# Attention and a gated feed-forward layer in two passes: two ff tiles moved to the second pass, with one pair of weights fetched again

## The chip, the cores and the metric

The kernel runs on one core of a Trainium2 chip. The metric is the device time of one launch in microseconds; three runs of the kernel before took 961.78, 963.28 and 963.41 us, with a median of 963.28 us.

## The reference

Causal attention with a window of 128 and a slope per head on q, k and v of shape (8, 8, 576, 64), whose output becomes 4608 rows of 512; then two matrix products with a gate between them. The weights come as float64.

```python
B, H, S, D = q.shape                              # 8, 8, 576, 64
scores = np.matmul(q, k.transpose(0, 1, 3, 2)) / np.sqrt(D)
bias = slopes[:, None, None] * (-np.abs(rel))[None]
scores = np.where((rel >= 0) & (rel < 128), scores + bias[None], -1e9)
attn = np.exp(scores - scores.max(-1, keepdims=True))
attn = attn / (attn.sum(-1, keepdims=True) + 1e-09)
x = np.matmul(attn, v).transpose(0, 2, 1, 3).reshape(B * S, H * D)
h = x @ w_in                                      # 512 by 2048
sp = np.maximum(h, 0.0) + np.log1p(np.exp(-np.abs(h)))
out = (h * erf(sp)) @ w_out                       # 2048 by 512
```

## The kernel before

The 4608 rows are cut into 12 chunks of 384 (`CH`), the 2048 columns of the ff dimension into 16 tiles of 128 (an ff tile, `f`). Matrix products of the second part are made of three products of rounded halves (high by high, high by low, low by high), so that each logical 128x128 product is three matmuls.

**Attention.** A unit is one chunk and two heads, 48 in all (`Attention.unit`). Its steps, each on the engine named: the scores on PE (L478, 24 matmuls on quarters of the array, 64 by 64); the bias, with a running minimum, on DVE (L505); the exponentials and their sums on ACT (L515); the inverse of the sums on DVE (L528, L529); the scaling on POOL (L538); the transposes on PE (L554); the copies of these to `pT` on DVE or ACT (L417, L415). For two units together the products with v are made on PE (L595, on quarters of the array too); they are rounded to the high half of `x` on DVE or ACT, and the rest is the low half, on DVE (L605). `save_x` writes `x` to DRAM (L776). In every third chunk (two remainders of 192 rows) the scores are four groups of heads and blocks of rows; there they go to three banks, with a drain of PE before the last group (L474, L475).

**First pass.** It makes ff tiles 0 to 5 (`NF1 = 6`) for each chunk as soon as its x is there, between the steps of the attention. One first-pass unit is one chunk and one ff tile, 72 in all: 12 matmuls to the bank `h` (L801), the copy to `hs` (L784, L786), and 9 matmuls to the banks `o` (L864). Two units (`UPR = 2`) make a round (`flush`): ACT loads the softplus table, then the erf table, then the table of the exponentials (L832, L834, L835); DVE multiplies, rounds and takes the rest (L843, L848). After a chunk's last tile its three sums are copied (L786) and parked in DRAM (L878).

**Second pass.** The ten ff tiles left are five pairs. Two chunks are taken together, so that there are six double chunks. A pair of tiles and a double chunk is a 2 by 2 product of blocks, made with seven block products instead of eight (`pair`, L1003, 42 matmuls, from sums and differences of x and of the weights) and 36 matmuls to six banks (L1074). `operands` loads x again and makes the sums (L918 to L936); `store` adds the sum of the first pass and writes the output (L886, L891).

**Weights.** `plain` turns float64 to float32 with integer operations on ACT and DVE (L636 to L649). The first pass's tiles are prepared into SBUF (`prepare`); those of the second pass are prepared during the attention as well, eleven tiles of 256 KB for a pair, and parked in DRAM (`spare_pair`, `spare_out`, buffers `wd`). When the attention's buffers are closed (`close`, L1136), they are fetched (`fetch`, L724) into the room that these leave, and into that of the first pass's weights (`take`).

**What sets the order.** Every step is an `op` with a due time `at`, a cost and the engines that can do it. `Plan.run` plays the program through with these costs and writes the instructions out in the order that comes of it: on each engine, the ready step with the earliest due time goes next (L292). `unit_time` gives the due time of an attention unit, `t0 + U * TM` that of a first-pass unit, `t1 + p * TP` that of a pair. The tables `UNITS`, `FIRST`, `TILES` and `KEPT` shift single steps. The order of each queue, SP's with the DMAs too, is therefore fixed before the run.

**PSUM.** Before there are four kinds of banks: three (`a`) for scores, transposes and products with v, two (`h`), and three (`o0` to `o2`), one for each 128 rows of a chunk. In the second pass `a` and `o` together hold the six sums.

```python
                for o in ready[e]:
                    if o.ready > t + self.WAIT[e] + 1e-9 or (best and (best.at, best.seq) < (o.at, o.seq)):
                        continue
                    if fits(o) and all(t + o.costs[e] <= max(free[x], t) + c for x, c in o.costs.items()):
                        best = o
```

Of the kernel before, what the change touches and what calls it, by code (L numbers as in the profile page):

```python
# [8 lines left out]
F32 = mybir.dt.float32  # L9
# [10 lines left out]
P = 128  # L20
# [22 lines left out]
TE, NE = 4, 6  # L43
TA = 6.5
LL, LN, LT, PXL = 26, 0, 0, 0.1
SQ = 0.36
LEAD = 45

TM = 4.8
TP = 13.0  # L50
XL = 60
MC, MP, MH = 4, 16, -16
W1A, W1B, W1C = 24, 6, 0.3
W2A, W2B, W2C = 40, 2.0, 0.5
WS, WSD, NWH = 140, 34, 2
HM, LM, PM = 0.2, 1.5, 0.4
W1R, NSV, GSV = 40, 5, 3
XP2, XD2 = 24, 4
TS, VL, NQF, SLP = 9, 8, 4, True
WB, PIE = "o1", 2  # L60
VE = -17
TURN = (0, 1, 2, 1, 2, 1, 2, 1)

UNITS = {16: 8, 17: 8, 18: 4, 19: 4, 20: 4, 21: 4, 22: 4, 23: 4, 24: 4, 25: 4, 26: 4, 27: 4, 28: 4, 29: 4, 31: 4, 10: -4, 11: -4, 12: -2, 13: -4, 14: -4, 15: 4, 7: -8, 8: -8, 9: -8, 37: 1, 38: 1, 39: 1, 40: 1, 41: 1, 42: 1, 43: 1, 44: 1}
FIRST = {41: -8, 67: 1, 68: 1, 69: 1, 70: 1, 71: 1, 52: -8, 2: 4, 3: 4, 4: 4, 5: 4, 6: 4, 7: 4, 8: 4, 9: 4, 10: 4, 11: 4, 12: 4, 13: 4, 14: 4, 15: 4, 16: 4, 17: 4}
TILES = {(0, 4): -2, (0, 5): -2, (1, 0): -2, (1, 1): -2, (1, 3): -2, (1, 4): -2, (1, 5): -2}
KEPT = {(1, 11): 12, (1, 12): 12, (1, 13): 12, (1, 14): 12, (1, 15): 12, (1, 8): -3}
# [47 lines left out]
class Plan:  # L115
# [15 lines left out]
    def __init__(self):  # L131
        self.ops = []
        self.slots = {}

    def op(self, costs, emit, r=(), w=(), at=0.0, moved=0, packet=0.0, after=0.0, rows=1.0, count=0, tail=0.0, port=False):
        o = Op()
        o.count, o.tail, o.packet, o.after, o.port, o.landed = count, tail, packet, after, port, False
        o.rows = rows
        o.costs, o.emit, o.at, o.seq, o.moved, o.lag = costs, emit, at, len(self.ops), moved, 0.0
# [30 lines left out]
    def run(self):  # L170
# [12 lines left out]
        placed = set()  # L183

# [17 lines left out]
        def on_pe(o, t):  # L202

            left = o.costs["PE"]
# [57 lines left out]
        while events:  # L262
# [92 lines left out]
def unit_time(u):  # L355
    return TE * min(u, NE) + TA * max(0, u - NE) + UNITS.get(u, 0)

# [859 lines left out]
```

## Time and profile before

| | |
|---|---|
| median of three runs | 963.28 us |
| the profiled execution, its own time | 963.49 us |
| its span | 961.6 us (1.9 us less than its time) |
| PE busy | 942.8 us, 98% of the span |
| DVE busy | 685.5 us, 71% |
| ACT busy | 662.2 us, 69% |
| POOL busy | 160.0 us, 17% |
| attention, from its first scores to its last product with v | 5.8 to 414.3 us |
| rest of the first pass alone | 414.3 to 476.0 us |
| second pass | 476.0 to 956.4 us |

The span runs from the first to the last instruction that the profile shows; the time of an execution holds 1.9 us more. A share of busy time is an average over stages: DVE's 71% is over 90% in the attention and near 56% in the second pass. The start of an instruction is measured, while the end of a matmul is modelled and runs into the next one; so what a group of matmuls costs is read from its start to the start of the next.

### The profile page before, as it was taken

How to read it: one execution, taken by the hardware profiler on the slowest of the kernel's cores; microseconds unless marked ns; L12 is line 12 of the kernel's file. 1: busy time of each engine (PE TensorE's matmuls, PEld its weight loads, DVE VectorE, ACT ScalarE, POOL GpSimd, SP SyncE). 2: the span in 40 equal slices, each digit the busy share in tenths (PEclk: the TensorE clock that was granted, in tenths of full speed). 3: DMA queues.
4: the chain of work that ended last, by engine and by line, in shares of the span. 5: the costliest groups of instructions: out<-in, count | busy, mean ns of one | idle time of the engine just before them, and what ended most of it. 6: DMA issues, size and time to landing. Idle time of an engine off the chain costs nothing.

```text
span 961.6 us, 18491 instructions
## 1 busy us (share of the span) xinstructions
PE 942.8 (98%) x6872; PEld 820.6 (85%) x6872; DVE 685.5 (71%) x1641; ACT 662.2 (69%) x1247; POOL 160.0 (17%) x300
## 2 busy tenths in 40 slices
PE   8799999999999999999999999999999999999997
PEld 7677887888888888799999899998989898989996
DVE  6999999989999897966474475556458267544533
ACT  6899889878988897977764644645463545465551
POOL 4623442433432343400000000000000000000000
PEclk9999999999999999999999999999999999999999
DMA  9743366678775575469554414225134052220302
GB/s 354 265 147 137 119 240 210 224 249 283 237 275 207 189 255 209 145 241 391 201 206 142 165 45 154 98 99 165 56 142 153 12 197 79 86 99 22 110 1 77
DMA packets 63082, 160.73 MB, mean 167 GB/s; under 512 B 7056, under 2 KB 11280, under 8 KB 62992
## 3 DMA queue, kind: packets, MB, share of 16 engines
q1 hardware_dynamic: 62848, 159.41, 47.2%
q8 instruction: 55, 0.90, 0.4%
q14 instruction: 35, 0.29, 0.1%
q10 hardware_dynamic: 144, 0.13, 0.1%
HBM read 107.35 MB, written 52.17 MB: 166 GB/s over the span
## 4 chain that ended last, share of the span: by engine, by line
PE 86%; DVE 9%; DMA 2%; ACT 2%; issue 1%; POOL 0%; DVEq 0%; ACTq 0%; POOLq 0%
PE o L864 13%; PE pa L1003 13%; PE h L801 13%; PE po L1074 13%; PE pa L1074 12%; PE pc L1003 7%; PE s L478 4%; PE px L595 4%; PE t L554 4%; PE pb L1003 3%; DVE p L505 2%; ACT p L515 1%; DVE pT L417 1%; DVE gl L848 1%; PE warm_ps L410 1%
## 5 line engine op out<-in xcount | busy, mean ns | idle before, releaser
L538 POOL TENSOR_SCALAR p<-p,st 128x192 f32<-128x192 f32 (+1 forms) x288 | 157.0, 564 | 243.3 <-DVE st L529 171.9
L801 PE MATMUL h<-x,wi 128*128 128x384 f32 x864 | 174.9, 346 | 0.8 <-ACT hs L784 0.8
L784 ACT COPY hs<-pa 128x384 f32<-128x384 f32 x92 | 44.1, 480 | 180.2 <-PE pa L1003 179.6
L801 PEld LDWEIGHTS h<-x,wi 128*128 128x128 f32 x864 | 151.6, 190 | 9.3 <-issue 3.1
L864 PE MATMUL o<-wo,gh 128*128 128x512 f32 x432 | 141.6, 409 | 0.0
L515 ACT ACTIVATE p<-p,st 128x192 f32<-128x192 f32 (+1 forms) x288 | 123.9, 432 | 16.9 <-DVE st L505 16.7
L1003 PE MATMUL pa<-t,p 128*128 128x384 f32 x540 | 108.9, 336 | 0.0
L1003 PEld LDWEIGHTS pa<-t,p 128*128 128x128 f32 x540 | 96.4, 188 | 5.9
L786 DVE COPY hs<-pa 128x384 f32<-128x384 f32 x28 | 15.6, 557 | 108.8 <-PE pa L1003 108.8
L1074 PE MATMUL po<-ho,gh 128*128 128x512 f32 x270 | 91.0, 391 | 0.0
L1074 PE MATMUL pa<-ho,gh 128*128 128x512 f32 x270 | 90.5, 389 | 0.0
L864 PEld LDWEIGHTS o<-wo,gh 128*128 128x128 f32 x432 | 74.9, 188 | 15.4 <-issue 6.1
L864 PE MATMUL o<-wo,gl 128*128 128x512 f32 x216 | 85.3, 395 | 0.0
L554 PE MATMUL t<-ident,p 128*128 128x128 f32 x400 | 64.5, 280 | 7.8 <-POOL p L538 5.0
L1014 DVE TENSOR_TENSOR hs<-pc,hs 128x384 f32<-128x384 f32 x60 | 33.3, 555 | 53.7 <-PE pc L1003 39.4
L1074 PE MATMUL po<-ho,gl 128*128 128x512 f32 x180 | 71.3, 396 | 0.0
L1054 DVE TENSOR_TENSOR hs<-s,hs 128x768 f32<-128x768 f32 x60 | 56.2, 950 | 20.9 <-ACT s L1046 20.9
L1074 PE MATMUL pa<-ho,gl 128*128 128x512 f32 x180 | 70.1, 389 | 0.0
L505 DVE CUSTOM_DVE_ANT_0 p<-s,bias 128x192 f32<-128x192 f32 x224 | 65.8, 349 | 1.4 <-PE s L478 1.0
L554 PEld LDWEIGHTS t<-ident,p 128*128 128x128 f32 x400 | 47.3, 142 | 22.2 <-POOL p L538 11.0
L478 PE MATMUL s<-qk 64*64 64x192 f32 (+1 forms) x1152 | 58.9, 323 | 4.2 <-issue 1.7
L1074 PEld LDWEIGHTS pa<-ho,gh 128*128 128x128 f32 x270 | 50.7, 188 | 10.9
(258 smaller groups left out, 1836.4 us busy)
## 6 DMA issues: line engine op xcount, KB each, us to landing
xd<-x SPq DMA_DIRECT2D x24, 768.0 KB, 4.8
qk<-qk_a SPq DMA_DIRECT2D x32, 416.0 KB, 4.6
pd<-ot SPq DMA_DIRECT2D x36, 256.0 KB, 3.5
out<-pd SPq DMA_DIRECT2D x36, 256.0 KB, 3.6
p<-wd SPq DMA_DIRECT2D x35, 256.0 KB, 5.2
wri<-w_in SPq DMA_DIRECT2D x16, 512.0 KB, 6.6
wro<-w_out SPq DMA_DIRECT2D x16, 512.0 KB, 4.4
qk<-qk_c SPq DMA_DIRECT2D x16, 512.0 KB, 4.4
```

The costliest lines, as they stand in the source:

```text
L478: nc.tensor.matmul(bank[h * D : (h + 1) * D, x : x + n], lhsT=q(t, j, h), rhs=k(j, off[h], n), start=True, stop=True)
L505: nc.vector.tensor_tensor_reduce(out=pt[:, c0:, j, :], in0=ps[j][0][:, ps[j][1] : ps[j][1] + n].rearrange("p (c d) -> p c d", d=D), in1=se ...
L515: nc.scalar.activation(dst, dst, AF.Exp, bias=low[t][:, j : j + 1], scale=-1.0, accum_out=sums[t][:, j : j + 1])
L538: nc.gpsimd.tensor_scalar(dst, dst, sums[t][:, j : j + 1], 1.0, op0=ALU.mult, op1=ALU.mult)
L554: nc.tensor.matmul(two[:, :, (2 - cb) * D : (3 - cb) * D], lhsT=p[t][:, cb].rearrange("p j d -> p (j d)"), rhs=self.ident[:, :], is_transp ...
L595: nc.tensor.matmul(px[j][cols, to : to + m * D], lhsT=v[rows, blk, :], rhs=pT[rows, src : src + 4 * m - 3 : 4, :], start=x == 0, stop=x + ...
L784: self.nc.scalar.copy(out, src)
L801: nc.tensor.matmul(ps[:, :CH], lhsT=ww[:, cs], rhs=xx[:, k], start=(k2 + k + n == 0), stop=(k2 + k + n == 4),)
L864: nc.tensor.matmul(po.all, lhsT=g[:, j, cs], rhs=w.all, start=(u["start"] and n == 0), stop=(u["end"] and n == 2),)
L1003: nc.tensor.matmul(dst[:, :CH], lhsT=wv[i](k), rhs=xb[l][:, k], start=start and k + n == 0, stop=k + n == 3, skip_group_check=not start)
L1054: op({"DVE": dve(2 * CH)}, lambda e, s=s, hs=hs: V.tensor_tensor(hs.all, s.all, hs.all, ALU.mult), r=[s, *parts], w=parts, at=at, port=True)
L1074: nc.tensor.matmul(po.all, lhsT=g[:, k, cs], rhs=w.all, start=start and n == 0, stop=end and n == 2)
```

## The change

- Four ff tiles stay in the first pass (48 units) and twelve go to the second (six pairs). A round is a chunk's four units (`UPR = 4`), and the products to `o` go by 128 rows: for each `t` both pairs of tiles, six matmuls in one step.
- There is room in SBUF for five pairs' weights. Pair 5 shares that of pair 2 (`TURNS`): in each double chunk pair 5's eleven tiles are fetched after pair 2 is done, and from the second on pair 2's again (`again`), `WF` ahead of their due time.
- Scores, transposes, products with v and `o` share one pool of six banks. The scores of the last chunk of three have a fourth bank, and the drain is gone.
- The planner takes scores and products with v that follow such a step up to `QB` earlier, and counts the change of the array's mode (`SQ`) only where it happens. The due times are new; the four tables are replaced by `SHIFT`.

```diff
-NF1 = 6
-FITP, FITO = 3, 5
-UPR = 2
+NF1 = 4
+FITP, FITO = 3, 9
+TURNS = {5: 2}
+UPR = 4
+NA, KO = 6, 2
...
-LEAD = 45
+QB = 20
+LEAD = 54
-TM = 4.8
-TP = 13.0
+TM = 7.45
+TP = 14.65
...
-            left = o.costs["PE"]
+            left = o.costs["PE"] + (SQ if o.quad and not inside else 0)
...
+                due = lambda o: (o.at - (QB if o.quad and inside else 0), o.seq)
                 for o in ready[e]:
-                    if o.ready > t + self.WAIT[e] + 1e-9 or (best and (best.at, best.seq) < (o.at, o.seq)):
+                    if o.ready > t + self.WAIT[e] + 1e-9 or (best and due(best) < due(o)):
...
-        ps = [bank(j) for j in range(2 + (last and len(ts) == 3))]
+        ps = [Buf(self.ps, [P, 512], F32, "a", NA, f"s{u}_{j}", keep=0) for j in range(4 if last else 2)]
...
-            for step, row in enumerate(zip(*todo)):
-                if len(ps) == 3 and step == 2:
-                    nc.tensor.drain()
+            for t, put, off, n in todo:
                 for h in range(2):
...
-            po = [Buf(self.ps_o, [P, DM], F32, f"o{t}", 1, f"o{t}_{self.U}") for t in range(NTT)]
+            po = [Buf(self.ps_a, [P, DM], F32, "a", NA, f"o{t}_{self.U}", keep=KO) for t in range(NTT)]
...
-            for j, u in enumerate(us):
-                self.products(u, j, gh, gl)
+            done.append((us, gh, gl))
         for t in range(NTT):
+            for us, gh, gl in done:
+                self.products(us, t, gh, gl)
...
+                if j in TURNS or (c and j in TURNS.values()):
+                    weights.again(j, time(c * npair + j) - WF)
                 self.pair(c, j, weights, x, new, at)
...
-    for j in range(npair):
+    own = [j for j in range(npair) if j not in TURNS]
+    for j in own:
         homes[2, j] = [take(j < FITP, f"p{j}_{i}") for i in range(7)]
...
+    def again(j, at):
+        i = TURNS.get(j, j)
+        homes[2, j] = [Buf(pool2, [P, DM], F32R, f"p{i}_{n}", 1, f"p{j}_{n}") for n in range(7)]
+        for k in range(2):
+            homes[1, NF1 + 2 * j + k] = [Buf(pool2, [P, DM], F32R, f"{x}o{NF1 + 2 * i + k}", 1, f"{x}o{NF1 + 2 * j + k}") for x in "hl"]
+        fetch(j, at, [gone])
```

How the change moves instructions, at three places, as the two programs hold them (names are tiles, with their buffer numbers; `x2` is two instructions alike).

ACT, one round of the first pass in the kernel before: `s` holds softplus and erf of two units' `hs`; L515 is the exponentials of an attention unit.

```order
L832 ACT_TABLE_LOAD
L832 ACTIVATE s_1876<-hs_1847 128x768
L834 ACT_TABLE_LOAD
L834 ACTIVATE s_1876<-s_1876 128x768
L835 ACT_TABLE_LOAD
L415 CAST x_0_1954<-px_1910 128x384
```

The same in the changed kernel, a round of four units:

```order
L837 ACT_TABLE_LOAD
L837 ACTIVATE s_3937<-hs_3678 128x768
L837 ACTIVATE s_3939<-hs_3835 128x768
L839 ACT_TABLE_LOAD
L839 ACTIVATE s_3937<-s_3937 128x768
L839 ACTIVATE s_3939<-s_3939 128x768
L840 ACT_TABLE_LOAD
```

Three table loads now serve two tiles `hs` where they served one: 36 loads in the first pass instead of 108.

PE, after the last product with v (`px`) in the changed kernel: `h` and `o` of the last two chunks, up to the second pass's first product, of which the first row stands last.

```order
L594 MATMUL px_5729<-pT_5704,v_5352 64x64
L805 MATMUL h_5771<-x_0_5088,wi_1149 128x384 x6
L805 MATMUL h_5771<-x_1_5334,wi_1149 128x384 x6
L872 MATMUL o_36_5789<-wo_1326,gh_5580 128x512 x2
L872 MATMUL o_36_5789<-wo_1326,gl_5657 128x512
...
L805 MATMUL h_5914<-x_1_5778,wi_1149 128x384 x6
L1014 MATMUL pa_0_5971<-11_0_5844,p_0_5860 128x384 x2
```

Between the first and the last of these rows the changed kernel has 60 matmuls to `h` and 42 to `o`; the kernel before has 174 and 135 at this place.

SP, in the second pass, at the end of the first double chunk, before: x of the next double chunk (`11`, `21`, `22`) is fetched from `xd`, then the plain blocks of the one after.

```order
L918 DMA rl21__1_7076<-xd2_1_73 128x768
L941 DMA 11_1_7191<-xd2_0_72 128x1536
L941 DMA 21_1_7199<-xd2_1_73 128x1536
L941 DMA 22_1_7261<-xd3_1_75 128x1536
L918 DMA rh11__2_7313<-xd4_0_76 128x768
```

The same place in the changed kernel:

```order
L927 DMA rl21__1_6667<-xd2_1_73 128x768
L950 DMA 11_1_6672<-xd2_0_72 128x1536
L950 DMA 21_1_6677<-xd2_1_73 128x1536
L727 DMA p2_0_6686<-wd2_2_0_183 128x512
L727 DMA p2_1_6690<-wd2_2_1_184 128x512
L727 DMA p2_2_6709<-wd2_2_2_185 128x512
L727 DMA p2_3_6713<-wd2_2_3_186 128x512
L727 DMA p2_6_6751<-wd2_2_6_189 128x512
L727 DMA p2_4_6756<-wd2_2_4_187 128x512
L727 DMA p2_5_6759<-wd2_2_5_188 128x512
L950 DMA 22_1_6783<-xd3_1_75 128x1536
```

Seven tiles of pair 2 have come in ahead of `22`; they overwrite pair 5's.

## Rows read from the trace of the kernel before

**Rows 1.** The page, its first part: busy time, share, instructions of each engine.

```profile
PE 942.8 (98%) x6872; PEld 820.6 (85%) x6872; DVE 685.5 (71%) x1641; ACT 662.2 (69%) x1247; POOL 160.0 (17%) x300
```

**Rows 2.** Busy times by stretch: those from 5.8 hold four attention units each.

```profile
core 0: us, PE busy (x) PEld busy (x) DVE busy (x) ACT busy (x) POOL busy (x), PEclk, DMA share, GB/s
5.80:20.70 14.90, 13.67 (x203) 10.85 (x202) 12.30 (x64) 13.28 (x57) 10.11 (x23) 1.00 1.04 406
20.70:57.50 36.80, 29.11 (x340) 23.86 (x341) 36.15 (x116) 29.55 (x79) 16.70 (x30) 0.95 0.75 280
57.50:91.70 34.20, 32.16 (x299) 25.44 (x299) 33.86 (x101) 33.10 (x69) 12.96 (x18) 0.95 0.30 106
91.70:125.90 34.20, 34.20 (x363) 28.25 (x362) 33.96 (x106) 30.67 (x83) 13.58 (x24) 1.00 0.39 133
...
373.20:414.30 41.10, 40.65 (x464) 33.47 (x463) 34.83 (x104) 35.84 (x81) 15.80 (x30) 1.00 0.51 182
414.30:476.00 61.70, 61.70 (x310) 55.89 (x310) 33.39 (x45) 48.64 (x53) 0.00 (x0) 1.00 0.73 266
476.00:956.40 480.40, 480.40 (x2395) 432.95 (x2394) 267.82 (x379) 256.53 (x321) 0.00 (x0) 1.00 0.31 107
...
0.00:424.40 424.40, 410.56 (x4220) 340.99 (x4221) 389.74 (x1225) 365.09 (x885) 160.00 (x300) 0.99 0.62 220
...
58.70:62.00 3.30, 3.30 (x16) 2.43 (x11) 3.30 (x16) 3.07 (x10) 0.00 (x0) 0.50 0.37 134
```

**Rows 3.** Timeline of PE, one first-pass unit: start, length, line, tiles, count.

```profile
442.55 2.27 PE L801 MATMUL h<-x,wi 128*128 128x384 f32 x12
444.65 0.63 PE L864 MATMUL o<-wo,gh 128*128 128x512 f32 x2
...
446.74 2.27 PE L801 MATMUL h<-x,wi 128*128 128x384 f32 x12
```

**Rows 4.** Timeline of PE, second pass: the first product of two successive pairs.

```profile
565.73 1.23 PE L1003 MATMUL pa<-11_1_7191,p 128*128 128x384 f32 x6
...
581.31 1.23 PE L1003 MATMUL pa<-11_1_7191,p 128*128 128x384 f32 x6
```

**Rows 5.** Timeline of PE: scores with the drain (first two rows), and without it.

```profile
62.96 1.55 PE L478 MATMUL s<-qk 64*64 64x192 f32 x24
64.44 3.40 PE L801 MATMUL h<-x,wi 128*128 128x384 f32 x18
...
91.39 0.39 PE L864 MATMUL o<-wo,gl 128*128 128x512 f32 x1
91.71 1.10 PE L478 MATMUL s<-qk 64*64 64x128 f32 x24
92.74 0.73 PE L864 MATMUL o<-wo,gh 128*128 128x512 f32 x2
93.30 0.39 PE L864 MATMUL o<-wo,gl 128*128 128x512 f32 x1
```

**Rows 6.** Groups of instructions by line: one table load; one low half.

```profile
L832 ACT ACT_TABLE_LOAD x36 | 46.2, 1283 | 1.7 <-DVE hs L786 1.1
...
L848 DVE TENSOR_TENSOR gl<-hs,gh 128x768 fp32r<-128x768 f32 x36 | 35.0, 973 | 0.8 <-ACT gh L784 0.4
```

**Rows 7.** Timeline of SP's queue around the end of the attention.

```profile
424.44 0.32 SPq L776 DMA_DIRECT2D xd<-x  x1
...
427.45 3.71 SPq L724 DMA_DIRECT2D p<-wd  x7
...
448.01 0.32 SPq L941 DMA_DIRECT2D 11_0_6492<-xd  x1
...
450.82 0.43 SPq L941 DMA_DIRECT2D 21_0_6512<-xd  x1
```

**Rows 8.** The page, DMA issues: count, KB each, us from issue to landing.

```profile
p<-wd SPq DMA_DIRECT2D x35, 256.0 KB, 5.2
```

**Rows 9.** Timeline of PE: twelve products to `h` ahead of the scores at 62.96.

```profile
59.20 3.83 PE L801 MATMUL h<-x,wi 128*128 128x384 f32 x12
```

More of the change, by code (lines that the diff above doesn't have):

```diff
@@ L133, in __init__, with op @@
         self.slots = {}
-    def op(self, costs, emit, r=(), w=(), at=0.0, moved=0, packet=0.0, after=0.0, rows=1.0, count=0, tail=0.0, port=False):
+        self.part = None
+    def op(self, costs, emit, r=(), w=(), at=0.0, moved=0, packet=0.0, after=0.0, rows=1.0, count=0, tail=0.0, port=False, quad=False):
         o = Op()
+        o.quad = quad
         o.count, o.tail, o.packet, o.after, o.port, o.landed = count, tail, packet, after, port, False
         o.rows = rows
+        o.part = self.part
+        at += SHIFT.get(self.part, 0)
         o.costs, o.emit, o.at, o.seq, o.moved, o.lag = costs, emit, at, len(self.ops), moved, 0.0
@@ L494, in unit @@
         p = [Buf(self.pp, [P, 3, 2, D], F32, "p", PB, f"p{u}_{t}") for t in range(3)]
-        for ts in ((0, 1), (2,)) if last and not WHOLE else ((0, 1, 2),):
-            self.scores(u, ts, q, k, list({id(b): b for t in ts for b in loaded[t]}.values()), early, p)
+        self.scores(u, q, k, list({id(b): b for bs in loaded for b in bs}.values()), p)
         for t in range(3):
@@ L579, in pair @@
         at = unit_time(u + 1) + LN + LT + PXL
-        px = [Buf(self.ps, [P, 512], F32, "a", 3, f"px{u + j}", keep=0) for j in range(2)]
+        self.plan.part = f"v{u}"
+        px = [Buf(self.ps, [P, 512], F32, "a", NA, f"px{u + j}", keep=0) for j in range(2)]
         terms = []
@@ L597, in products @@
                             start=x == 0, stop=x + 1 == len(terms))
-        op({"PE": SQ + sum(2 * max(m * D / 1200 + 0.002, 0.06) for _, _, m, _ in terms)}, products,
-           r=[b for v, _, parts in units for b in (v, *parts)], w=px, at=at)
+        op({"PE": sum(2 * max(m * D / 1200 + 0.002, 0.06) for _, _, m, _ in terms)}, products,
+           r=[b for v, _, parts in units for b in (v, *parts)], w=px, at=at, quad=True)
         for j in range(2):
@@ L662, in prepare @@
     def prepare(self, which, f, at):
+        self.plan.part = f"w{which}_{f}"
         pool, tag = self.place(which, f)
@@ L790, in unit @@
         U = self.U
+        self.plan.part = f"h{U}"
         wh, wl = w.t[0, f]
@@ L822, in flush @@
         V, A = nc.vector, nc.scalar
-        pairs = []
+        pairs, done = [], []
+        self.plan.part = f"g{units[0]['U']}"
         for k in range(0, len(units), 2):
@@ L899, in operands @@
         V = nc.vector
+        self.plan.part = f"x{c}"
         x, plain = {}, {}
@@ L1038, in flush2 @@
         at += MC
+        self.plan.part = f"b{ts[0]['c']}_{ts[0]['j']}{ts[0]['half']}"
         for t in ts:
@@ L1064, in products2 @@
         c, j, half = tile["c"], tile["j"], tile["half"]
+        self.plan.part = f"c{c}_{j}{half}"
         for t in range(NTT):
```

128 lines of the change are left out of this document (64 added, 64 removed).

## The prediction

> **What bounds the kernel now.** I read the page first: PE is busy for 98% of the span, DVE for 71%, ACT for 69% [rows 1]. That looks like a kernel bound by PE alone, but a share over the whole span is a mean over stages, so the second view is the busy times by stretch [rows 2]. There the reader sees three kernels in one. From 476.0 on (second pass) PE is busy all the time and DVE for 56%: PE alone is the bound. From 414.3 to 476.0 (what is left of the first pass) likewise. Before 414.3 the attention runs too, and there PE, DVE and ACT are all near their limit: in the stretch from 57.5 to 91.7 they are busy for 32.2, 33.9 and 33.1 of 34.2 us. DVE is the bound up to about 126, PE after it. So what the change takes off PE is worth its full price in the last two stages; in the attention it is worth only what the next engine lets through.
>
> To get at that I counted, in the order of each engine, the instructions between the scores of every fourth attention unit, priced each at its group's time from start to start, and took the busiest engine of each stretch. For the kernel before this gives 15.3, 36.3, 34.4, 34.3 us for the first four stretches; the rows say 14.9, 36.8, 34.2, 34.2. The eleven stretches up to the scores of unit 44 add up to 367.4 us by the count, and the trace has 5.8 to 373.2, also 367.4. The last, to the end of the last product with v, comes to 39.1 against 41.1 measured. So the rule "a stretch lasts as long as its busiest engine" holds here within 2 us in 408, and I use it for the changed kernel.
>
> **The change, part by part.**
>
> *Fewer products on PE.* A first-pass unit takes 446.74 - 442.55 = 4.19 us of PE [rows 3]; a pair of the second pass takes 581.31 - 565.73 = 15.58 us [rows 4]. Two ff tiles in 12 chunks are 24 units, 100.6 us, that go; one pair in six double chunks, 93.5 us, comes (seven block products for eight). PE does 7.1 us less.
>
> *The drain.* Scores of the third kind of chunk take 64.44 - 62.96 = 1.48 us with their drain, others 92.74 - 91.71 = 1.03 [rows 5]. The former have 2304 columns to 2048, so without a drain some 1.16 us (an estimate by columns; between 1.03 and 1.48): 16 x 0.32 = 5.1 us less.
>
> *The array's mode.* Going into scores costs 91.71 - 91.39 = 0.32 us where a product takes 0.23, and coming out costs 93.30 - 92.74 = 0.56 for two products that take 0.46 elsewhere [rows 5, 3]: 0.2 us for each run of scores and products with v. The order has 53 such runs for 70: 3.4 us less. With that, PE alone would save 15.6 us.
>
> *DVE, ACT.* Up to the last low half of x, DVE's order loses 52.9 us of work: 17 gate instructions and 10 rounded halves (a low half is 0.97 us in its group [rows 6]), 21 copies of `hs`, 15 of sums, 33 of transposes and 5 roundings of x, most of which ACT takes over; one more parked pair adds 7, and four tiles fewer prepared in SBUF take away 4. ACT loses 57 table loads of 1.28 us [rows 6], 73 us, and with those copies is 59.5 us shorter. These have no price of their own; they set the stretches below. A load has 1.7/36 = 0.05 us of idle time ahead of it [rows 6], so I price it at 1.28. The Trainium skill (ScalarE: Activation LUTs, What ACT_TABLE_LOAD costs) agrees on the load, but adds a drain of 1.38 us to every switch. By that the 31 loads left would cost ACT 43 us more, it would be the busiest engine of several stretches, and the sum would come some 8 us higher, an estimate; the idle time in rows 6 speaks against it.
>
> *The attention.* The same count for the changed kernel gives, as the busiest engine of each stretch, 14.6 (ACT), 15.1, 21.8, 22.0 (DVE), 40.1 (PE), 31.1 (DVE), 27.8 (ACT), 47.6 (PE), 31.5, 24.6, 33.2 (DVE) and 38.9 (PE): 348.4 us for the 408.5 of before. DVE, not PE, is now the bound of most. With the start at 5.8 the last product with v ends at 354.2. POOL has 13 us in each stretch and decides none.
>
> *Rest of the first pass.* 60 products to `h` and 42 to `o`, for 174 and 135 in 61.7 us [rows 2]. At 2.10/12 and 2.09/9 us [rows 3] that is 20.2 us (the same prices give 61.8 for before).
>
> *Second pass.* 36 x 15.58 = 560.9, and the 54 products to `o` that are left in it, 12.5. The same sum for before is 479.9 and the row says 480.4, so I add 0.5: 573.9. Behind the last product lie 961.6 - 956.4 = 5.2 us, unchanged.
>
> *What I cost at nothing.* The weights fetched again: 11 times eleven tiles of 0.26 MB, 32 MB, some 60 GB/s more in a stage that moves 107 and where 266 has been moved beside a full PE [rows 2]. A tile of pair 5 can come when pair 2 has read it; that leaves two pairs, 31 us, to land in, and a tile lands in 5.2 us [rows 8]. Without that cover each fetch would cost up to 2.9 MB / 266 GB/s = 10.8 us. DVE's and ACT's work of the sixth pair lies beside PE, which leaves them over 40% idle there. The six shared banks: of PE's 13.8 us of idle time up to 424.4 some 11 lie in the first three stretches [rows 2], so banks can win next to nothing; a loss is in the range. The longer round on ACT (7 us for 5.5) delays exponentials, but nine buffers `p` stand between.
>
> *Sum.* 5.8 + 348.4 + 20.2 + 573.9 + 5.2 = 953.5 us of span, for 961.6. The profiled execution took 1.9 us more than its span and was 0.2 above the median of the runs: 955.4 us, 8 below the median. Its own range, with 2 us of the rule's error and 0.3 us more or less in each stretch, is 950 to 961.
>
> **The rivals.**
>
> *The stretches level out* (faster still). If the engines run ahead from one stretch to the next, only the totals count. DVE has 389.7 - 52.9 = 336.8 us of work up to the last low half [rows 2]; its idle time was 9 us up to 91.7 and would stay that. That half would end at 346, the product with v 1.7 us before it at 344.3, 9.9 earlier: 945.5. For it: DVE had gaps of 1.2 us in all from 20.7 to 125.9 [rows 2]. Against: PE and ACT have 95% and 90% of DVE's work, and each waits for the others in a fixed order.
>
> *Level engines lose* (no change). The two stretches in which DVE was fullest, from 20.7 and 57.5, lost 0.65 and 0.34 us beyond its work [rows 2]; the rule has that in its 2 us of error once. At 0.65 more in each of twelve, 7.8 us: 963.2. For it: the changed stretches have two or three engines within 5% of each other.
>
> *The second pass begins late* (slower). Its first products need x and weights that can only come when the attention's buffers are closed. Before, SP issued the last save at 424.44, weights from 427.45, x at 448.01 and 450.82 [rows 7], for a start at 476: 61.7 us behind the last product with v, now 20.2. If the loads took as long as before (450.82 + 5.2 - 414.3 = 41.7), PE would wait 21.5 us: 976.9. It decides from 10 us on. SP is a queue, and in it two parked sums stand ahead of what the second pass needs, and wait for products to `o` 5 to 9 us behind the last product with v. Against: only two loads of x and two tiles are needed at first, 2.1 MB, 8 us at 266 GB/s, and in the new order they stand first; I see some 6 us to spare.
>
> *PE's clock falls* (slower). From 20 to 79 us PE now has 12.1, 19.8 and 15.7 us of work in stretches of 15.1, 21.8 and 22.0. Before, the granted clock was 0.50 of full, 1.2 for 2.4 GHz, from 58.7 to 62.0 [rows 2], and twelve products took 62.96 - 59.20 = 3.76 us for 2.10 [rows 9, 5, 3]; PE had been idle for 7.7 of 36.8 us before that. At the lower level all through, PE would be the bound of the three stretches, with twice its work, 36 us more; at the lower level half of the time 12.5 more, 967.9. It decides from nearly half of the time on. Against: PE is busy for 71 to 91% there, and was for 79% in the stretch from 20.7, with 0.95 of the clock.
>
> *The reload holds up SP* (slower). Behind seven tiles of pair 2 stands the load `22`; if it, or the tiles fetched again, came 2 us late at each of the 11 reloads, 22 us: 977.4. Against: the tiles are free 11 us into pair 5, and `22` is read 11 us into the next pair, 10 us after it can have landed.
>
> **How the numbers follow.** Forecast 0.54; levelling out 0.22; no change 0.12; a late start 0.06; the clock 0.04; the reload 0.02. Under 0.2% (2 us) a measurement of this kernel cannot tell from no change. The first two are faster, 0.76; the third is the same, 0.12; the last three slower, 0.12. For 8 in 10 the range begins at 946, in the upper half of the second case, and ends at 964, behind the third.
>
> **What would show it.** In the changed profile: pairs of 15.6 us; scores of 1.16 us in every third chunk; the last product with v near 354, the second pass from 374 on, without a gap before its first product; DVE over 93% up to 340. A gap on PE at 374, a clock under 0.9 before 65, or idle time on PE in the second pass would make the prediction wrong upwards; a last product with v before 346, downwards.

## The result and the profile after

The changed kernel took 955.18 us (median of four runs, 954.64 to 956.12), the kernel before on the same chip 963.35 (four runs, 961.78 to 964.44): a ratio of 0.9918, with a 95% interval of 0.9900 to 0.9935. The prediction was 955.4.

The page's first part, which answers to [rows 1]:

```profile
PE 928.5 (97%) x6836; PEld 817.5 (86%) x6836; DVE 653.6 (69%) x1578; ACT 620.1 (65%) x1276; POOL 177.8 (19%) x300
```

PE has 14.3 us less to do, but the span is only 8.2 us shorter (953.4 for 961.6): PE's idle time rose from 18.8 to 24.9 us. DVE lost 31.9 us over the whole span and ACT 42.1. POOL gained 17.8, with as many instructions as before; nothing in the prediction speaks of that gain.

The busy times by stretch answer to [rows 2]; here the stretches are those of the prediction, from the scores of every fourth unit to the next, then the rest of the first pass and the second, and last all up to the last low half of x.

```profile
core 0: us, PE busy (x) PEld busy (x) DVE busy (x) ACT busy (x) POOL busy (x), PEclk, DMA share, GB/s
...
19.90:36.50 16.60, 13.59 (x203) 10.21 (x192) 16.46 (x75) 14.59 (x60) 9.93 (x23) 1.00 0.89 336
...
74.10:118.00 43.90, 41.50 (x422) 35.15 (x413) 42.97 (x136) 40.81 (x112) 19.86 (x30) 1.00 0.64 228
118.00:147.40 29.40, 27.85 (x329) 23.66 (x328) 29.26 (x92) 26.38 (x71) 12.54 (x18) 1.00 0.81 280
...
221.20:253.30 32.10, 30.84 (x309) 26.02 (x312) 31.27 (x92) 25.21 (x63) 11.93 (x18) 1.00 0.71 234
...
310.70:355.20 44.50, 39.78 (x466) 33.73 (x465) 38.30 (x108) 32.02 (x87) 24.95 (x35) 1.00 0.57 211
355.20:375.40 20.20, 20.20 (x107) 18.45 (x104) 12.27 (x17) 12.39 (x16) 0.00 (x0) 1.00 0.79 280
375.40:949.30 573.90, 573.90 (x2863) 517.36 (x2862) 306.84 (x433) 308.14 (x388) 0.00 (x0) 1.00 0.45 161
0.00:356.90 356.90, 336.12 (x3882) 283.38 (x3883) 335.38 (x1130) 300.02 (x873) 177.82 (x300) 1.00 0.77 271
```

Three things are to be seen. The last two stages came out as forecast: 20.2 us and 573.9, PE busy throughout, with 161 GB/s beside it for the 107 of before. In the attention DVE is the fullest engine of most stretches (16.46 of 16.6, 29.26 of 29.4). And the last stretch is another case: no engine fills its 44.5 us, and PE, the fullest, stands still for 4.7.

The two kernels' attention side by side, from the same view: 408.5 us with PE busy 395.7 and DVE 383.5 before; 349.0 with PE 329.3 and DVE 333.6 now. The bound went over from PE to DVE. PE's idle time in it rose from 12.8 to 19.7 us, and what grew is the part that ends with a scaling of `p` on POOL (who waited for whom: us in total, times, longest; before, then now):

```profile
PE t L554 <- POOL p L538: 5.0, 9, 1.7
PE t L552 <- POOL p L537: 12.7, 20, 1.7
```

How the second pass begins, in PE's timeline and SP's queue [rows 7]:

```profile
374.33 1.23 PE L805 MATMUL h<-x,wi 128*128 128x384 f32 x6
375.40 1.20 PE L1014 MATMUL pa<-11_0_5844,p 128*128 128x384 f32 x6
376.44 1.20 PE L1014 MATMUL pb<-21_0_5857,p 128*128 128x384 f32 x6
```

```profile
356.93 0.32 SPq L779 DMA_DIRECT2D xd<-x  x1
357.49 0.32 SPq L950 DMA_DIRECT2D 11_0_5844<-xd  x1
363.17 0.32 SPq L886 DMA_DIRECT2D pd<-ot  x1
363.54 0.43 SPq L950 DMA_DIRECT2D 21_0_5857<-xd  x1
364.01 0.45 SPq L727 DMA_DIRECT2D p<-wd  x1
```

SP stood for 5.4 us between the issue of `11` (357.49 and 0.32) and that of the parked sum at 363.17, as the rival of the late start had it, and `21` went out behind it at 363.54, 12.9 us before its product at 376.44. So of the two loads of x only `11` stood first, where the prediction has both. It was early enough all the same: no gap stands before the first products.

### The profile page after: what moved, and what is told of

Same layout as the page of the kernel before. It is cut to its first block, busy times and chain, and to the rows that moved or that the text cites. A ratio compares the mean times of both kernels' runs of the same rounds, so it can differ in the third digit from the quotient of the medians.

```text
span 953.4 us, 18648 instructions
## 1 busy us (share of the span) xinstructions
PE 928.5 (97%) x6836; PEld 817.5 (86%) x6836; DVE 653.6 (69%) x1578; ACT 620.1 (65%) x1276; POOL 177.8 (19%) x300
## 4 chain that ended last, share of the span: by engine, by line
PE 79%; DVE 10%; POOL 4%; ACT 2%; issue 2%; DMA 2%; POOLq 0%; SPq 0%; DVEq 0%
PE po L1087 31%; PE pa L1014 16%; PE pc L1014 8%; PE h L805 6%; PE o L872 6%; PE pb L1014 4%; POOL p L537 4%; PE px L594 3%; PE s L478 2%; PE t L552 2%; DVE p L504 2%; ACT p L514 1%; DVE pT L423 1%; DMA wd<-wto 1%; DVE x L604 1%
## 5 line engine op out<-in xcount | busy, mean ns | idle before, releaser
L537 POOL TENSOR_SCALAR p<-p,st 128x192 f32<-128x192 f32 (+1 forms) x288 | 174.8, 628 | 168.8 <-ACT p L514 62.3
L1087 PE MATMUL po<-ho,gh 128*128 128x512 f32 x468 | 176.3, 389 | 0.0
L1087 PE MATMUL po<-ho,gl 128*128 128x512 f32 x432 | 169.7, 393 | 0.0
L1087 PE MATMUL po<-lo,gh 128*128 128x512 f32 x396 | 155.4, 392 | 0.0
L805 PE MATMUL h<-x,wi 128*128 128x384 f32 x576 | 117.7, 347 | 0.0
L805 PEld LDWEIGHTS h<-x,wi 128*128 128x128 f32 x576 | 97.8, 188 | 5.1 <-issue 3.9
L1087 PEld LDWEIGHTS po<-ho,gh 128*128 128x128 f32 x468 | 87.8, 188 | 14.4
L1087 PEld LDWEIGHTS po<-ho,gl 128*128 128x128 f32 x432 | 81.0, 188 | 17.1
L872 PE MATMUL o<-wo,gh 128*128 128x512 f32 x288 | 92.3, 401 | 1.5 <-DVE wo L658 0.7
L1087 PEld LDWEIGHTS po<-lo,gh 128*128 128x128 f32 x396 | 74.3, 188 | 12.0
L552 PE MATMUL t<-ident,p 128*128 128x128 f32 x400 | 64.1, 280 | 16.6 <-POOL p L537 12.7
L1070 DVE TENSOR_TENSOR gl<-hs,gh 128x768 fp32r<-128x768 f32 x72 | 67.4, 953 | 0.6
```

The source lines that it names most:

```text
L537: nc.gpsimd.tensor_scalar(dst, dst, sums[t][:, j : j + 1], 1.0, op0=ALU.mult, op1=ALU.mult)
L552: nc.tensor.matmul(two[:, :, (2 - cb) * D : (3 - cb) * D], lhsT=p[t][:, cb].rearrange("p j d -> p (j d)"), rhs=self.ident[:, :], is_transp ...
L805: nc.tensor.matmul(ps[:, :CH], lhsT=ww[:, cs], rhs=xx[:, k], start=(k2 + k + n == 0), stop=(k2 + k + n == 4),)
L872: nc.tensor.matmul(po.all, lhsT=g[:, j, cs], rhs=w.all, start=(u["start"] and n == 0), stop=(u["end"] and n == 2),)
L1070: op({"DVE": dve(2 * CH)}, lambda e, gh=gh, gl=gl, hs=hs: V.tensor_tensor(gl.all, hs.all, gh.all, SUB), r=[*parts, gh], w=[gl], at=at, por ...
L1087: nc.tensor.matmul(po.all, lhsT=g[:, k, cs], rhs=w.all, start=start and n == 0, stop=end and n == 2)
```

## The experiments

In every run below the kernel before ran on the same chip (963.6 to 964.2 us); ratios are to it. "Theory 1" is the prediction's rule: a stretch lasts as long as its busiest engine.

**Stretch by stretch.** The lengths that the text below speaks of, each read from PE's timeline (start of the scores of every fourth unit to the next; the last to the end of the last product with v; where the trace has two units' scores in one row, a window printed below can begin or end some 0.2 us off the border):

| stretch | counted | changed kernel | two more loads a round | no addition | two units on ACT as well |
|---|---|---|---|---|---|
| 1 | 14.6 | 13.7 | 13.7 | 13.4 | 13.4 |
| 2 | 15.1 | 16.6 | 16.6 | 15.7 | 15.7 |
| 3 | 21.8 | 21.7 | 21.7 | 21.4 | 21.4 |
| 4 | 22.0 | 16.0 | 16.0 | 15.5 | 15.5 |
| 5 | 40.1 | 43.9 | 46.5 | 43.2 | 42.8 |
| 6 | 31.1 | 29.4 | 32.4 | 28.9 | 28.8 |
| 7 | 27.8 | 23.0 | 23.0 | 22.6 | 22.4 |
| 8 | 47.6 | 50.8 | 52.6 | 51.1 | 50.6 |
| 9 | 31.5 | 32.1 | 35.8 | 31.2 | 31.8 |
| 10 | 24.6 | 24.4 | 25.0 | 23.9 | 23.5 |
| 11 | 33.2 | 33.0 | 33.2 | 32.9 | 32.6 |
| 12 | 38.9 | 44.5 | 48.6 | 44.4 | 40.2 |
| attention | 348.4 | 349.0 | 365.1 | 344.2 | 338.6 |

**1. Two more table loads in each round.**

```diff
             for us, n, n2, hs, s, at in pairs:
                 A.activation(s[:, :n], hs[:, :n], AF.Softplus)
-            for us, n, n2, hs, s, at in pairs:
                 A.activation(s[:, :n], s[:, :n], AF.Erf)
```

> Edit: in a round of the first pass, softplus and erf alternate by tile hs, so that a round loads five tables instead of three; every engine's order is otherwise that of the changed kernel. ACT gets 12 x 2 x 1.28 = 30.8 us more work, 9 of the 12 rounds between the first scores and the last product with v. Theory (a stretch lasts as long as its busiest engine): in the changed kernel's trace ACT rises from 14.7 to 17.3 us in the fourth stretch (DVE 15.8), 40.8 to 45.9 in the fifth (DVE 43.0), 44.4 to 49.5 in the eighth (PE 48.7), 21.4 to 24.0 in the tenth (DVE 23.7), 30.8 to 33.3 in the eleventh (DVE 32.8) and stays below the others elsewhere: 1.5 + 3.0 + 0.8 + 0.3 + 0.5 = 6 us, 961. Rival 1 (PE alone sets the time, ACT has room): 0, 955. Rival 2 (the fixed order passes every delay on): 9 to 11 rounds x 2.6 = 23 to 28 us, 978 to 983. Rival 3 (every switch also drains ACT for 1.38 us, as the Trainium skill has it in ScalarE: Activation LUTs): 5.3 us a round, by the same count some 28 us, 983, with ACT idle for over a microsecond ahead of each load.

Measured: 977.57 us, ratio 1.0138 (1.0124 to 1.0151), 21 us behind the changed kernel's ratio. The span grew by 20.2, of which 16.1 lie in the attention, 1.4 in the rest of the first pass and 1.9 in the second. Theory 1's figure is far too low, the rivals' are nearest. Two stretches of this kernel, fifth and sixth, and the loads in its groups of instructions (count, busy, mean ns of one, idle time before):

```profile
75.20:121.60 46.40, 41.98 (x419) 35.19 (x410) 43.47 (x135) 45.23 (x115) 19.70 (x30) 1.00 0.61 214
121.60:154.00 32.40, 28.55 (x329) 23.58 (x328) 29.17 (x91) 31.61 (x74) 12.39 (x18) 1.00 0.76 256
```

```profile
L837 ACT ACT_TABLE_LOAD x24 | 30.8, 1283 | 0.4
L838 ACT ACT_TABLE_LOAD x24 | 30.8, 1283 | 0.4
```

The chain of work that ended last, followed back to its start, by engines: the changed kernel's and this one's.

```profile
PE 79%; DVE 10%; POOL 4%; ACT 2%; issue 2%; DMA 2%; POOLq 0%; SPq 0%; DVEq 0%
```

```profile
PE 70%; ACT 17%; DVE 6%; POOL 2%; issue 2%; DMA 1%; POOLq 0%; SPq 0%; ACTq 0%; DVEq 0%
```

ACT is now the fullest of both stretches, and its share of the chain went from 2% to 17%. In the sixth the count gave it 26.4 + 2.6 = 29.0 us; it has 31.6, since work that came late in the fifth was carried over. The fullest engines of stretches five to twelve add up to 9.8 us more than in the changed kernel, for 16 measured: the rest is new waiting, above all in the eighth, ninth and twelfth, where no engine is full, and PE's waits for a scaling of POOL went from 12.7 to 19.2 us. (Of the 9.8, 2.4 lie in the twelfth, where PE's granted clock stood at 0.50 for 3.4 us from 327.6 on; the changed kernel has 1.00 there.) So the rule is blind to this: in a fixed order a block of ACT that runs longer than the order allows for holds up what stands behind it, though the mean has room. Rival 3 falls with the fence of the loads: 0.4 us of idle time ahead of 24 loads is 0.02 each, no drain of over a microsecond.

**2. The drain put back.**

```diff
             for t, put, off, n in todo:
+                if last and t == 2:
+                    nc.tensor.drain()
```

> Edit: the drain of PE ahead of the last group of scores is put back in every third chunk (16 times), order unchanged. Between the 1.48 us with a drain in the kernel before and the 1.03 to 1.14 of the same scores in the changed kernel lie 0.35 to 0.45 us, 5.6 to 7.2 us of PE in all, 1.4 to 1.8 in each of the four stretches concerned. Theory (busiest engine): PE stands 0.7, 1.4 and 0.4 us below DVE in the third, sixth and ninth stretch and 1.5 above it in the last: 0.9 + 0.2 + 1.2 + 1.6 = some 4 us, 959, two thirds of the work added. Rival 1 (PE alone sets the time): 5.6 to 7.2, 961 to 962. Rival 2 (hidden everywhere, the attention waits for DVE, ACT and POOL): under 1, 955 to 956.

Measured: 960.69 us, ratio 0.9963 (0.9950 to 0.9975), 4.3 us behind the changed kernel's ratio. PE's timeline in the last chunk:

```profile
314.04 0.88 PE L480 MATMUL s<-qk 64*64 64x192 f32 x16
315.09 0.56 PE L480 MATMUL s<-qk 64*64 64x192 f32 x8 [0.16 <-DVE st L529]
315.57 0.44 PE L554 MATMUL t<-ident,p 128*128 128x128 f32 x2
```

From 314.04 to 315.57 are 1.53 us; the same scores in the changed kernel run from 310.74 to 311.87, 1.13. Sixteen times 0.40 is 6.4 us of PE, of which the time shows 4.3, two thirds. Theory 1 had 4.

**3. Nothing fetched again.**

```diff
     def again(j, at):
-        i = TURNS.get(j, j)
...
+        w2.pair[j] = w2.pair[TURNS.get(j, j)]
         for k in range(2):
...
-        fetch(j, at, [gone])
+            w2.t[1, NF1 + 2 * j + k] = w2.t[1, NF1 + 2 * TURNS.get(j, j) + k]
```

> Edit: no weights are fetched again; pair 5 multiplies by the weights of pair 2, which leaves out 121 loads of 256 KB (the sums of the sixth pair are then those of other weights). Theory (the reload lies beside PE and costs nothing): second pass 573.9 us as before, 954.5 to 956. Rival (the 32 MB cost something, by contention or by SP's queue): faster by 1 to 10 us, with the gain in the second pass.

Measured: 956.11 us, ratio 0.9920 (0.9907 to 0.9934). The second pass:

```profile
375.70:949.60 573.90, 573.90 (x2864) 517.39 (x2862) 306.62 (x432) 309.76 (x389) 0.00 (x0) 1.00 0.31 106
```

106 GB/s for 161 and the same 573.9 us: the reload costs nothing.

**4. The scaling of the last four units on ACT, with the planner told of it.**

```diff
+                        if e == "Act":
+                            nc.scalar.activation(dst, dst, AF.Copy, scale=sums[t][:, j : j + 1])
+                            continue
...
-                op({"Pool": 2 * (0.24 + (3 - c0) * D * 0.00086)}, scaled, r=[p[t], sums[t]], w=[p[t]], at=at)
+                op({"Act": 2 * act((3 - c0) * D)} if u >= 44 else {"Pool": 2 * (0.24 + (3 - c0) * D * 0.00086)}, scaled, r=[p[t], sums[t]], w=[p[t]], at=at)
```

> Edit: the scaling of p of the last four attention units goes from POOL to ACT. In the last stretch of the changed kernel PE is busy 39.8 of 44.5 us, and its four gaps (1.10, 1.73, 0.61, 1.28) all end with a p of POOL. Theory (POOL's slow scaling holds up the last stretch; ACT has 32.0 us of work there and gets some 7 more): the stretch falls to 40 to 42 us, 951 to 953. Rival 1 (the order of ACT, whose round of tables stands ahead of the last exponentials, sets it, and POOL is only the last link): 0 to -1, 954 to 955. Rival 2 (ACT becomes the bound of the stretch): 956 to 958.

Measured: 956.18 us, ratio 0.9918 (0.9905 to 0.9931), no change. The order was made anew by this edit: the last stretch took 46.7 us, the rest 19.1 and the second pass 572.4, and that stretch holds 66 products to `h` and 54 to `o` for the 60 and 48 of before. So products went from the later stages into it, and the run tells nothing apart; the last experiment does it without a new order.

**5. No tables in the first pass.** Theory 2, that any load on ACT still costs, came out of the first experiment.

```diff
-                A.activation(s[:, :n], hs[:, :n], AF.Softplus)
+                A.activation(s[:, :n], hs[:, :n], AF.Copy)
...
-                A.activation(s[:, :n], s[:, :n], AF.Erf)
-            A.preload_act_table_set(LOG_EXP_SET)
+                A.activation(s[:, :n], s[:, :n], AF.Copy)
```

> Edit: in the first pass softplus and erf are replaced by plain copies on ACT, so that its 36 table loads fall away (the first pass's gate is not computed; order and all else as in the changed kernel). In the ten rounds that lie in the attention ACT loses 10 x 3.85 = 38.5 us. Theory 1 (busiest engine per stretch): ACT is nowhere the busiest where a round lies, so nothing changes, 954 to 956. Theory 2, formed after the kernel with two loads more a round came out 20 us longer (16.5 of it in the attention, 0.64 us for each us of load): a round holds up the exponentials queued behind it on ACT, and with them POOL, the transposes and PE, however free ACT is on the mean. Then the loads that are left still cost time: up to 0.64 x 38.5 = 25 us, but no more than DVE's 335 us of work up to the last low half lets through, some 8 to 15: 940 to 947.

Measured: 955.80 us, ratio 0.9913 (0.9899 to 0.9926). No stretch differs from the changed kernel's by more than 0.2 us, though ACT has 40 us less to do in the attention (297.5 there in the changed kernel):

```profile
6.80:356.10 349.30, 329.42 (x3846) 276.45 (x3845) 333.96 (x1126) 257.10 (x839) 174.88 (x290) 1.00 0.77 272
```

Theory 1 holds and theory 2 falls: the loads that are left cost no time. With the first experiment this bounds ACT's slack: a round may end 3.85 us earlier for nothing, and may not end 2.57 us later.

**6. Rounds of two units again.** `UPR = 4` becomes `UPR = 2`; the planner makes its order anew.

> Edit: two units to a round again (UPR 2) in the changed kernel, the planner makes its order anew. 36 more table loads, 46 us on ACT, some 38 of it in the attention; a round takes 5.5 us instead of 7.2. Theory 1 (busiest engine): ACT becomes the busiest of stretches four to six, eight, ten and eleven, by 2.7 + 5.5 + 1.0 + 3.4 + 1.6 + 1.8 = 16 us, 971. Theory 2 (the loads hold up what is queued behind them, 0.64 us for each us): 0.64 x 38 = 25, 980. Rival (what costs is the length of one round, and shorter rounds make up for their number): 955 to 960.

Measured: 963.85 us, ratio 0.9994 (0.9985 to 1.0003): all of the gain is gone. Up to the first product of the second pass, this kernel and the changed one:

```profile
0.00:388.80 388.80, 367.20 (x4004) 308.53 (x4005) 363.08 (x1185) 347.24 (x898) 164.70 (x300) 0.98 0.76 264
```

```profile
0.00:375.40 375.40, 354.62 (x3975) 300.13 (x3976) 346.08 (x1144) 311.93 (x888) 177.82 (x300) 1.00 0.77 273
```

ACT has 35 us more and not 46, and DVE 17 more: over the whole span DVE has 1610 instructions for 1578, and ACT, with 36 more loads, only 4 more, so that 32 copies and roundings went back from ACT to DVE. That is how the longer round pays, as far as this run shows it: loads saved on ACT become copies that DVE, the bound, is rid of. The loss is some 7 us by the ratios. Theory 1's 16 are neither borne out nor refuted by it: the attention is 16.5 us longer, but it holds more products (24 to `o` are left to the second pass for 54), and the stages behind it are 8.8 us shorter. PE's granted clock was 0.50 for 13.6 us in three places of this attention, where the changed kernel has 1.00 throughout. DVE is the fullest engine of each of the four stretches concerned (36.8 of 36.9 us in the sixth); whether the clock took a part in the loss was not tried.

**7. The split alone undone.** `NF1 = 6`, `TURNS = {}`, `FITO = 5`, `UPR = 6`, `TM = 4.97`.

> Edit: the split alone undone in the changed kernel: six ff tiles in the first pass, five pairs and no reload in the second, a round a chunk of six units, due times of the first pass scaled to it; the planner makes its order anew. Theory (the second pass and the rest of the first are bound by PE, the attention is not made shorter by products taken from it but filled less): PE does 7.1 us more products and has its 20 us of idle time in the attention or less: 958 to 963. Rival 1 (more products to fill the attention's gaps make up for it): 952 to 957. Rival 2 (DVE and ACT get the gates of 24 units back in the attention, which is bound by them): 965 to 980.

Measured: 970.42 us, ratio 1.0062 (1.0050 to 1.0075), 14 us behind the changed kernel's ratio; rival 2's range.

**8. One round a chunk alone, in the kernel before.** `UPR = 2` becomes `UPR = 6` there.

> Edit: the kernel before with UPR 6 alone, one round a chunk instead of three; 72 table loads fall away, 92 us of ACT's 365 up to 424, its own tables of due times as they were. PE's idle time there was 13.8 us, 11 of it in the first three stretches. Theory 1 (busiest engine): before, PE and DVE bound every stretch and ACT none but the first, so 961 to 964. Theory 2 (loads hold up exponentials): the gaps of PE behind 57 us, about 5, can close, 957 to 961. Rival (a round of six units blocks ACT for some 9 us at once where one of two took 5.5, and the order was made for short rounds): slower, 965 to 985.

Measured: 976.11 us, ratio 1.0124 (1.0111 to 1.0138). Up to the second pass, this kernel and the one before:

```profile
0.00:489.50 489.50, 465.23 (x4479) 385.77 (x4480) 394.62 (x1204) 340.34 (x916) 174.64 (x300) 1.00 0.64 223
```

```profile
0.00:476.00 476.00, 462.16 (x4478) 387.63 (x4479) 417.02 (x1262) 405.71 (x927) 160.00 (x300) 0.99 0.64 228
```

65 us less on ACT, 22 less on DVE, and 13.5 longer, which is the rival's range: lighter engines alone are worth nothing with due times that were made for short rounds. Of the 13.5, 10.4 are new idle time of PE (13.8 before, 24.3 here), and its waits for a scaling of POOL went from 5.0 to 13.1.

**9. Split and round both undone.** As the seventh, with `UPR = 2`.

> Edit: six ff tiles in the first pass and two units a round in the changed kernel, that is both the split and the round undone, with shared banks, no drain and the new planner kept. It is the fourth corner beside the changed kernel (4 tiles, one round a chunk: 955), UPR 2 (4 tiles, rounds of two: 964) and the split undone (6 tiles, one round a chunk: 970). If split and round add up: 970 + 9 = 979. If a round a chunk pays only with four units in it (a round of four takes ACT some 7 us at once, one of six 9): 960 to 968, as the kernel before with its 963, less what banks, drain and mode give (5 us at most).

Measured: 964.34 us, ratio 1.0005 (0.9995 to 1.0015). The four corners, with shared banks, no drain and the new planner, as ratios to the kernel before:

| | two units a round | one round a chunk |
|---|---|---|
| six ff tiles in the first pass | 1.0005 | 1.0062 |
| four | 0.9994 | 0.9918 |

In these orders the split alone gains 0.1%, the round alone loses 0.6%, and together they gain 0.9%. Banks, drain and planner alone gain nothing against the kernel before, though the drain by itself cost 4.3 us in the second experiment. All four corners run with the changed kernel's due times (`TM` alone is scaled); what the other three would give with due times of their own was not tried.

**10. Nine microseconds less for DVE, order kept.**

```diff
             def inverse(e, both=both):
-                nc.vector.tensor_scalar(both(), both(), 1e-9, None, op0=ALU.add)
                 nc.vector.reciprocal(both(), both())
```

> Edit: the addition of 1e-9 to the sums of the exponentials (one small DVE instruction a unit, 48 in all, 9.3 us in the trace; a sum is never below 1 and 1e-9 is less than half of its last place, so it does not change it) is left out; order and planner's costs as in the changed kernel. It is the counterpart to the run without table loads, on the engine that the theory holds for the bound. Theory 1 (busiest engine per stretch): 0.78 us less for DVE in each stretch, of which PE lets through 0.8, 0.7, 0.2, 0.8, 0.8, 0.6, 0.0, 0.4, 0.5 in stretches two to ten: 4.7 us, 950 to 952. Theory 3 (with the order fixed, work that ends early gains nothing, on whatever engine): 0 to -1, 954 to 956.

Measured: 950.61 us, ratio 0.9856 (0.9842 to 0.9870); by the ratios 6 us ahead of the changed kernel, give or take 2; the profiled span fell by 4.6 us, the attention by 4.8, all of it but 0.2 in stretches one to ten, and none in the eighth. The rule had 4.7, with nothing in the eighth, the eleventh and the twelfth. Two of its stretches, the second and the fourth:

```profile
20.20:35.80 15.60, 13.32 (x200) 10.22 (x188) 15.60 (x71) 13.92 (x56) 8.88 (x22) 1.00 0.93 345
...
57.30:72.90 15.60, 15.60 (x249) 14.04 (x252) 15.60 (x62) 14.38 (x40) 10.22 (x20) 1.00 0.47 142
```

DVE is still full in both, so its missing work is missing time. Against the fifth experiment this is the plainest evidence for what bounds the attention: 40 us off ACT gave nothing, 9 us off DVE gave 4.7.

**11. The same with the planner told.** Its cost for the step goes from 0.315 to 0.19.

> Edit: the same, and the planner is told of it, so that the order is made anew (47 runs of scores and products with v instead of 53, 1.2 us of PE at 0.2 each). Theory 1: as above and 1 us more, 949 to 951. Theory 3 (the order decides): between 945 and 965, wherever the new order happens to stand; a fall beyond 6 us or a rise is not to be had from 9.3 us of DVE and 1.2 of PE and would be the order's.

Measured: 957.36 us, ratio 0.9925 (0.9911 to 0.9939), 6.8 us behind the tenth run with the same work. That is what one order is worth against another, and the trace shows where: up to the second pass PE has 1.9 us more to do and 5.5 more idle time, and five gaps of PE from 69.8 to 82.5, 7.5 us, all end with POOL's scaling of `p`. The greater part of that time:

```profile
72.70:82.90 10.20, 5.17 (x20) 3.72 (x20) 9.09 (x16) 4.76 (x15) 10.20 (x12) 0.67 0.00 0
```

POOL is busy throughout, and PE's granted clock, with PE idle for half of the time, is 0.50 from 72.7 to 79.5. The sixth, seventh and ninth runs, whose orders were made anew too, are to be read with that much in doubt, and the corners' share of it stays open.

**12. Two units' scaling on ACT, order kept.** On top of the tenth:

```diff
                     for j in range(2):
                         dst = p[t][:, c0:, j, :]
+                        if u in (43, 47):
+                            nc.scalar.activation(dst, dst, AF.Copy, scale=sums[t][:, j : j + 1])
+                            continue
                         nc.gpsimd.tensor_scalar(
```

> Edit: as the run without the addition of 1e-9 in the unchanged order, and the scaling of p of units 43 and 47 is issued to ACT where the order has it for POOL; nothing else is moved, unlike in the run in which the planner was told of such a change. In that run's last stretch PE was idle 0.98, 2.17 and 1.28 us ahead of transposes, each time for a p of POOL, which took 10.4 us for units 42 and 43 and 6.9 for unit 47; on ACT the six instructions of a unit take 6 x 0.47 = 2.8 us. Theory (POOL's scaling is on the path there, and the planner's new order, not ACT, ate the gain before): the gaps of 2.17 and 1.28 close, 2 to 3.5 us, 947 to 949. Rival 1 (what waits is put down to POOL but ends with DVE's inverse or ACT's exponentials): 0 to -1, 950 to 951. Rival 2 (ACT's own queue is late by these 5.6 us): 951 to 955.

Measured: 945.39 us (942.98 to 945.96), ratio 0.9808 (0.9794 to 0.9821): faster than both kernels, 18 us below the one before; the span is 5.2 us shorter than the tenth run's. Here is its last stretch, and after it the same stretch of the changed kernel, where PE's four gaps (idle time in brackets) all end with POOL:

```profile
305.60:345.70 40.10, 39.13 (x466) 34.04 (x465) 36.31 (x102) 35.25 (x99) 13.52 (x23) 1.00 0.62 233
```

```profile
313.41 0.55 PE L552 MATMUL t<-ident,p 128*128 128x128 f32 x3 [1.10 <-POOL p L537]
...
318.80 0.55 PE L552 MATMUL t<-ident,p 128*128 128x128 f32 x3 [1.73 <-POOL p L537]
...
347.62 0.55 PE L552 MATMUL t<-ident,p 128*128 128x128 f32 x3 [0.61 <-POOL p L537]
...
351.16 0.55 PE L552 MATMUL t<-ident,p 128*128 128x128 f32 x3 [1.28 <-POOL p L537]
```

With the two units on ACT, PE is busy for 39.1 of 40.1 us; one gap of 0.97 us is left. Against the tenth run the stretch fell by 4.2, a little more than the two gaps of 2.17 and 1.28 that were to close there.

## Why the prediction was right, and where it was not

**The sum.** Start 5.8, measured 6.2; attention 348.4, measured 349.0; rest of the first pass 20.2, measured 20.2; second pass 573.9, measured 573.9; tail 5.2, measured 4.1. The two stages that PE alone bounds came out within 0.2 us, as products priced from start to start should, and the pairs take 15.6 us as before. That the total fits so closely is luck: start and attention came out 1.0 us too long together, the tail 1.1 too short. By its own words the forecast was 955.2, for the profiled execution stood 0.2 us above the median and that was not taken off.

**What makes the attention shorter.** Right: DVE bounds most of it now (335.4 us up to the last low half, 336.8 forecast), it was relieved because ACT took copies over, and ACT could because loads fell away. The sixth run shows that chain backwards, the tenth and the fifth that DVE and not ACT is the bound. PE's 15.6 us "alone" were 14.3 in busy time, and 6.1 of them went into new idle time, 14.3 - 6.1 = 8.2.

**The rule stretch by stretch.** The sum was right by 0.6 us; the terms were not. The fourth stretch was counted at 22.0 and took 16.0, the fifth 40.1 and took 43.9, the seventh 27.8 for 23.0, the eighth 47.6 for 50.8. The 2 us of error that I took from the kernel before were those of its sum; "0.3 us more or less in each stretch" was not true of single stretches. A likely reason, not tested: the engines' orders do not cross a stretch's border at the same time, so what one stretch is short of the next has too much. The sum of the fullest engines as measured, 337.4, leaves 11.6 us of waiting that the count had in the wrong places.

**The last stretch.** The step that failed is "POOL has 13 us in each stretch and decides none": 38.9 us counted, 44.5 taken. POOL had 25 us in that stretch, and its scaling stood in PE's way; the twelfth run takes it out and the stretch falls to 40.2. This is what the rival of level engines forecast, at one place, though not for the reason given there. The other eleven stretches came to 304.5 us for 309.5 counted, and so hid it in the sum.

**The drain.** Mis-sized: scores without it were put at 1.16 us and take 1.03 to 1.14 with the change of mode, and 0.40 us a group hang on it, not 0.32. Put back it costs 4.3 us, so it was not merely "PE alone".

**Edits costed at nothing.** The reload: right, shown by the third run. The longer round on ACT: its nine buffers do cover it (fifth run), but with less than 2.57 us to spare (first run); I named the cover and not its size.

**Rivals.** Levelling out did not come: the stretches kept 11.6 us of waiting. The second pass did not begin late, though SP was held up. The clock did not fall: 1.00 in every stretch, where the kernel before had 0.95 in two [rows 2]; in the new orders of the sixth and eleventh runs it did. The reload held nothing up. The Trainium skill's rule of a 1.38 us drain for every switch (ScalarE: Activation LUTs, What ACT_TABLE_LOAD costs) would have made the first run's loads dearer than the 1283 ns that they show; the trace does not agree, with 0.02 us of idle time ahead of one.

**Not settled.** How much of the gain is the split's, the round's and the new order's apart from each other: two orders of the same work differ by 7 us. That the change of mode was worth 3.4 us was not tried.

## What to carry to other kernels

Count each engine's work by stages and you have the sum, but test it by taking work off one engine at a time with the order kept: here 40 us off one engine gave nothing and 9 us off another gave 5. In a program whose order is fixed beforehand, slack is one-sided: work that ends early gains nothing off the bound, work that ends late is passed on, and an edit that makes the order anew brings several microseconds of its own, so a small gain is best issued into the old order. And an engine that is idle for half of the time can still be the last link before the bound: look at what ends the bound's gaps, not at its share.

## What the runs showed of the hardware

POOL's scaling of `p` depends on what DVE does beside it. Six instructions of one unit took 3.03 us at 321.36 and 6.88 at 344.23 in the changed kernel; DVE's timeline beside the second, and a stretch of it beside a quick one (six in 3.46 us from 327.69):

```profile
321.36 3.03 POOL L537 TENSOR_SCALAR p<-p,st 128x192 f32<-128x192 f32 x6 [2.62 <-DVE st L528]
327.69 3.46 POOL L537 TENSOR_SCALAR p<-p,st 128x192 f32<-128x192 f32 x6 [3.30 <-PE s L478]
...
344.23 6.88 POOL L537 TENSOR_SCALAR p<-p,st 128x192 f32<-128x192 f32 x6 [1.63 <-ACT ot L787]
```

```profile
328.85 0.35 DVE L504 CUSTOM_DVE_ANT_0 p<-s,bias 128x192 f32<-128x192 f32 x1
...
344.79 0.69 DVE L648 TENSOR_TENSOR wto<-wto,wqo 128x512 f32<-128x512 f32 x1
345.39 1.10 DVE L848 TENSOR_TENSOR hs<-s,hs 128x768 f32<-128x768 f32 x1
346.41 0.94 DVE L936 TENSOR_TENSOR rh__0_5170<-rh__0_5170,rh__0_4989 128x768 f32<-128x768 f32 x1
```

In the slow case DVE runs instructions with two operands in SBUF, one after the other; in the quick one mostly the bias step, of whose operands one is in PSUM. Over all 288 scalings of the changed kernel, set against DVE's instructions running at the same time: 0.44 us in the mean for the 137 that met no such instruction, 1.46 for the 28 that had such ones beside them for over 90% of their time; in the kernel before 0.42 (181) and 1.23 (18). All 28 end 0.15 to 0.21 us behind the end of such an instruction of DVE: in the slow case the first two scalings end at 345.69 and 347.56, DVE's `wto` and `rh__0_5170` in the fence at 345.48 and 347.35. So such a scaling ends only once DVE's instruction has ended. The change put more of them beside such work, 151 for 107 met at least some, and that is the larger part of why the same instructions kept POOL busy for 174.8 us instead of 157.0 (their times added up: 180.8 for 162.4; the changed kernel's means with the 107 of before would give 165). The Trainium skill (SBUF — State Buffer, SBUF: two separate sides) says that DVE, with two inputs from SBUF, and GpSimd lock each other out of a pair of ports that they share. The trace agrees, with 1.46 us for 0.44.

Nor had I expected ACT's slack to end so sharply: two more loads in a round cost 21 us, and none at all gained nothing.
